# Moving the cluster similarities of the next head pair into the middle of each attention turn

## The chip, the cores and the metric

The kernel runs on one core of a Trainium2 chip. The metric is the device time of one execution in microseconds (us). A core has five engines that each work through their own instruction list in order and meet through semaphores: TensorE (PE in the profile, with its weight loads as PEld), VectorE (DVE), ScalarE (ACT), GpSimd (POOL) and SyncE (SP, which here only starts transfers). Three executions of the kernel before took 701.83, 703.33 and 704.82 us; the median is 703.33 us. The profiled execution spans 687.2 us on the core's own clock; the rest of a measured time lies outside that span.

## The reference

Two blocks in sequence. The attention block groups queries and keys by the nearest of 16 normalised centroids, and lets a query see only the keys of its own cluster. The second block sends every token to one of 8 experts.

```python
B, H, S, D = 4, 8, 768, 64            # 16 clusters
q_assign = argmax(einsum('bhsd,hcd->bhsc', q_n, c_n), -1)     # the clusters
k_assign = argmax(einsum('bhsd,hcd->bhsc', k_n, c_n), -1)
mask = q_assign[:, :, :, None] == k_assign[:, :, None, :]
scores = where(mask, q @ k.T / sqrt(D), -1e9)
attn = softmax(scores) ; x = (attn @ v) -> rows of (B*S, H*D) = (3072, 512)

logits = x @ w_gate                    # 8 experts, one per token
expert = argmax(logits) ; gate_w = softmax(logits)[expert]
y = gate_w * (relu(x @ w1[expert]) @ w2[expert])              # F = 1024
```

Everything is float32 at the inputs and the output.

## The kernel before

The attention works on 16 pairs of heads, called g = 0 to 15 (4 batches, 4 pairs each). One pair is one **turn** of the main loop. A turn has 12 units (2 halves of the queries, 6 blocks of keys). First come the 12 scores of the turn, then the point called `mid`, then the 12 products with V (`attend`), then the point called `end`. Other work is hung in at named places: `at(g, mid, f, ...)` means that `f` is written into the instruction lists at the middle of turn g; `at(g, 5, ...)` after score number 5; `at(g, UG + 5, ...)` after attend number 5 (UG is 12). Every engine runs its list in that order.

```python
def similar(g):                       # similarities of pair g to the 16 centroids
    ps = ps_o.tile(...) if g == 1 else wide()[:, 0, :]
    for t in range(4): nc.tensor.matmul(ps[32 rows of t, 0:384], lhsT=cblk[...], rhs=qk[g][...])
    sims[g] = ...; nc.vector.transpose(sims[g], ps[:, 0:HS])

def assign(g):                        # largest similarity, first of equals (1st part)
    nc.vector.tensor_reduce(mx, sim, op=max)
    nc.vector.tensor_tensor(sim, sim, mx, op=is_ge)
    (nc.gpsimd if g > 1 else nc.vector).tensor_tensor(sim, sim, first_c, op=mult)

def assign2(g):                       # 2nd part: a one-hot of the cluster
    nc.vector.tensor_reduce(top, rank, op=max)
    nc.vector.tensor_tensor(oh, rank, top, op=is_equal)
    nc.vector.transpose(sims[g], oh)

def put_by_scalar(g):                 # one-hots to the operand that masks the scores
    for half in range(2):
        for a in range(2):
            nc.scalar.copy(ohT[g][..., 0, cols], t[i])
            nc.scalar.activation(ohT[g][..., 1, cols], t[k], AF.Identity, scale=..., bias=...)

def score(u):                         # 12 per turn
    ps = ps_s.tile([P, 2, 512])       # pool of 3, also used by wide()
    2 matmuls (float32) of k and q  ; 2 matmuls (bf16) of ohT add the mask
    A[u] = ap.tile(...)               # pool of 12
    nc.scalar.activation(A[u], ps, AF.Exp, scale=D**-0.5)
    if g == NG - 2 and u % UG >= 3: later_sums.append((u, A[u]))   # turn 14 only
    else: add_up(u, A[u])             # T += A on VectorE; 10 instructions for 12 units

def attend(u):  2 matmuls (float32) O += v . A[u]
def finish(g, half):  nc.scalar.copy(XT[g][half], O)
def weigh(g):   # sums of weights (from T) and gate logits (from XT), 12 small matmuls, then VectorE and GpSimd
def keep(g, c0, c1):  nc.vector.transpose(xb, XT[g]); four stores of rows by GpSimd's queue
def turn_blocks(g):   two VectorE transposes of q and k
def choose(pool, part):  # 5 VectorE instructions: expert of every token
def count(part):         # 2 small matmuls of the result of choose, then a VectorE copy
def slots1 / one_hots1(i):   # places of the tokens, on VectorE (and GpSimd)
def tokens1 / spread1:   # small matmuls, then VectorE: the row numbers to gather
def turn_rows1(i):       # VectorE: divide and transpose the gathered rows (tile xu)
def first_half(0, ...):  # first expert matmuls, read xu; start after weigh(15)
...
at(-1, end, turn_blocks, 1)
for f in (similar, assign, assign2): at(0, 4, f, 1)
for g in range(NG):
    at(g, end, finish, g, 0) ; at(g, end, finish, g, 1)
    if g + 2 < NG:
        at(g, mid, turn_blocks, g + 2)
        at(g, end, similar, g + 2) ; at(g, end, assign, g + 2)
    if g < NG - 1:
        at(g, end, keep, g, 0, S) ; at(g + 1, mid, weigh, g)
        at(g, mid, put_by_scalar, g + 1)
    if g + 2 < NG: at(g, end, assign2, g + 2)
    if g % HP == HP - 1 and g < NG - 1:      # HP = 4: after each batch
        at(g + 1, mid, gate, g // HP) ; at(g + 1, end, gate2, g // HP) ; ...
at(12, end, choose, pl, front) ; at(13, mid, count, front)
at(13, end, slots1) ; at(13, end, one_hots1, 0) ; at(13, end, one_hots1, 1)
at(14, UG + 3, tokens1) ; at(14, UG + 3, sums_of_later, 2)
at(14, UG + 6, spread1) ; at(14, UG + 6, gather1, 0) ; at(14, UG + 6, sums_of_later, UG)
at(15, mid, gather1, 1) ; at(15, mid, turn_rows1, 0)
at(16, mid, weigh, 15) ; ... at(16, mid, first_half, 0, 0, FB // 4)
```

So before the change the similarities of pair g + 2 are made at the end of turn g, and their one-hots are put in place in the middle of turn g + 1: a whole turn lies between them and the scores that need them.

Of the kernel before, what the change touches and what calls it, by code (L numbers as in the profile page):

```python
# [8 lines left out]
F32 = mybir.dt.float32  # L9
# [3 lines left out]
AF = mybir.ActivationFunctionType  # L13
# [172 lines left out]
def kernel(  # L186
# [11 lines left out]
    nc = tc.nc  # L198
    B, H, S, D = q.shape
    C = centroids.shape[1]  # L200
    P = 128
# [4 lines left out]
    NG = B * HP  # L206
# [27 lines left out]
    def fetch1(e, i):  # L234
        w1 = wpool.tile([P, DB, F], F32, name=f"w1_{i % 2}")
        nc.sync.dma_start(out=w1, in_=moe_w1[bass.ds(e, 1)].rearrange("e (a p) f -> p (e a) f", p=P))
        return w1

    def fetch2(e, i):
        w2 = wpool.tile([P, FB, Dm], F32, name=f"w2_{i % 2}")  # L240
        nc.sync.dma_start(out=w2, in_=moe_w2[bass.ds(e, 1)].rearrange("e (a p) d -> p (e a) d", p=P))
        return w2
# [24 lines left out]
    ps_o = late.enter_context(tc.tile_pool(name="ps_o", bufs=2, space=PSUM))  # L267
# [9 lines left out]
    def wide():  # L277
        return pools["s"].tile([P, 2, 512], F32, name="sps")
# [4 lines left out]
    def bank():  # L283

        return wide()[:, 0, :] if "attention" in pools else ps_o.tile([P, 512], F32, name="O")
# [332 lines left out]
    for name, t0, n in (("f", 0, NF), ("b", NF, NQ)):  # L618
# [4 lines left out]
            keep=rte.tile([P, E, n], F32, name="keep_" + name),  # L623
# [112 lines left out]
    with ExitStack() as actx:  # L736
# [9 lines left out]
        pl = actx.enter_context(tc.tile_pool(name="places1", bufs=1))  # L746
# [54 lines left out]
        big = consts.tile([P, 2, 2], F32)  # L801
# [14 lines left out]
        ps = bank()  # L816
# [15 lines left out]
        for i in range(2):  # L832
            t = ohp.tile([P, 2, S], BF16, name=f"ohT{i}")
            nc.gpsimd.memset(t, 0.0)
            ohTs.append(t)
        for a in range(2):
            r = slice(a * D, (a + 1) * D)
# [31 lines left out]
        qk, sims, ohT = {}, {}, {}  # L869
# [37 lines left out]

        def similar(g):


            ps = ps_o.tile([P, 512], F32, name="O") if g == 1 else wide()[:, 0, :]
            for t in range(4):
                w, half = divmod(t, 2)
                nc.tensor.matmul(  # L914
                    ps[t * 2 * C : (t + 1) * 2 * C, 0:HS], lhsT=cblk[:, g % HP].rearrange("p a c -> p (a c)"),
                    rhs=qk[g][:, w, half * HS : (half + 1) * HS], start=True, stop=True,
                )


            sims[g] = asg.tile([P, HS], F32, name="sim")  # L920
            nc.vector.transpose(sims[g], ps[:, 0:HS])

        def groups_of(t):
            return t.rearrange("p (t c) -> p t c", c=C)

        def assign(g):

            sim = groups_of(sims[g])
            mx = asg.tile([P, G], F32, name="mx")
            nc.vector.tensor_reduce(mx, sim, axis=AX, op=ALU.max)  # L930
            nc.vector.tensor_tensor(sim, sim, mx.unsqueeze(2).to_broadcast([P, G, C]), op=ALU.is_ge)  # L931
            (nc.gpsimd if g > 1 else nc.vector).tensor_tensor(  # L932
                sim, sim, first_c[:, None, :].to_broadcast([P, G, C]), op=ALU.mult
            )

# [12 lines left out]
        def places(half, a):  # L948

            return slice(half * 32, half * 32 + 32), slice(a * D, a * D + 32), slice(half * HS, (half + 1) * HS)  # L950

        def put_by_scalar(g):

            t = sims.pop(g)
            ohT[g] = ohTs[g % 2]
            for half in range(2):
                for a in range(2):
                    i, r, cols = places(half, a)
                    k = slice(D + half * 32, D + half * 32 + 32)
                    nc.scalar.copy(ohT[g][r, 0, cols], t[i])  # L960
                    nc.scalar.activation(  # L961
                        ohT[g][r, 1, cols], t[k], AF.Identity, scale=big[k, a, 0:1], bias=big[k, a, 1:2]
                    )

        def put(g):

# [19 lines left out]
        A, T, O = {}, {}, {}  # L986
        XT = {}

        def where(u):
            g, r = divmod(u, 2 * NQ)  # L990
            return g, r // NQ, r % NQ

        def score(u):
            g, half, j = where(u)
            qs = slice(half * HS, (half + 1) * HS)
            ks = slice(j * P, (j + 1) * P)
            ps = ps_s.tile([P, 2, 512], F32, name="sps")
            for a in range(2):
                r = slice(a * D, (a + 1) * D)
                nc.tensor.matmul(ps[:, a, 0:HS], lhsT=qk[g][r, 1, ks], rhs=qk[g][r, 0, qs], start=True, stop=False)  # L1000
            for a in range(2):
                r = slice(a * D, (a + 1) * D)
                nc.tensor.matmul(ps[:, a, 0:HS], lhsT=ohT[g][r, 1, ks], rhs=ohT[g][r, 0, qs], start=False, stop=True)  # L1003
            A[u] = ap.tile([P, 2, HS], F32, name="A")
            nc.scalar.activation(A[u], ps[:, :, 0:HS], AF.Exp, scale=D**-0.5)  # L1005
            if g == NG - 2 and u % UG >= 3:
                later_sums.append((u, A[u]))
            else:
                add_up(u, A[u])
# [3 lines left out]
        def add_up(u, a_u):  # L1013
            g, half, j = where(u)
            if j == 0:
                last_a[0] = a_u
            elif j == 1:
                T[g, half] = tp_.tile([P, 2, HS], F32, name="T", bufs=4)
                nc.vector.scalar_tensor_tensor(
                    T[g, half], in0=last_a[0], scalar=1e-9 / P, in1=a_u, op0=ALU.add, op1=ALU.add  # L1020
                )
            else:
                nc.vector.tensor_tensor(T[g, half], T[g, half], a_u, op=ALU.add)  # L1023
# [110 lines left out]
        def at(n, part, f, *a):  # L1134
            jobs.setdefault((n, part), []).append((f, a))

        UG = 2 * NQ
# [3 lines left out]
        mid, end = "mid", "end"  # L1141
# [3 lines left out]
        at(-4, mid, load_next)  # L1145
        at(-4, end, turn, 0, 1)
        at(-3, mid, similar, 0)
        at(-3, mid, assign, 0)
        at(-3, mid, assign2, 0)
        at(-3, mid, put, 0)  # L1150
        at(0, 2, put_q, 0, 1)
        at(-2, end, idle_of, 20)
        at(-1, end, turn_blocks, 1)
        for f in (similar, assign, assign2):
            at(0, 4, f, 1)
        for g in range(NG):
            at(g, end, finish, g, 0)
            at(g, end, finish, g, 1)
            if g + 2 < NG:
                at(g, mid, turn_blocks, g + 2)  # L1160
                at(g, end, similar, g + 2)
                at(g, end, assign, g + 2)
            if g < NG - 1:
                at(g, end, keep, g, 0, S)
                at(g + 1, mid, weigh, g)
                at(g, mid, put_by_scalar, g + 1)
            if g + 2 < NG:
                at(g, end, assign2, g + 2)
            if g % HP == HP - 1 and g < NG - 1:
                at(g + 1, mid, gate, g // HP)  # L1170
                at(g + 1, end, gate2, g // HP)
                at(g + 1, end, keep_pads, g // HP)


        front = parts[0]
# [39 lines left out]
            layer1(g, (f0, f1))  # L1215

        n = NG - HP
        at(n, end, choose, pl, front)
        at(n + 1, mid, count, front)
        at(n + 1, end, slots1)  # L1220
        at(n + 1, end, one_hots1, 0)
        at(n + 1, end, one_hots1, 1)

        at(n + 2, UG + 3, tokens1)
        at(n + 2, UG + 3, sums_of_later, 2)
        at(n + 2, UG + 6, spread1)
        at(n + 2, UG + 6, gather1, 0)
        at(n + 2, UG + 6, sums_of_later, UG)
        at(n + 3, mid, gather1, 1)
        at(n + 3, mid, turn_rows1, 0)  # L1230

        n = NG
# [35 lines left out]
        for n in range(-4, NTURN + 2):  # L1268
            for i, x in enumerate(range(n * NB, (n + 1) * NB)):
                if 0 <= x < NU:  # L1270
                    score(x)
                run(n, i)
            run(n, mid)
            for i, x in enumerate(range(n * NB, (n + 1) * NB)):
                if 0 <= x < NU:
                    attend(x)
                run(n, NB + i)
            run(n, end)
# [8 lines left out]
    with tc.tile_pool(name="sm", bufs=1) as sm:  # L1287
        front, back = parts
# [19 lines left out]
        for part in parts:  # L1308
            n, over = part["n"], part["over"]
# [95 lines left out]
    g = groups[0]  # L1405
# [61 lines left out]
    with tc.If(more > 0):  # L1467
        nx = nc.values_load(xe[0:1, NX : NX + 1], min_val=0, max_val=NX)
        general = nc.values_load(xe[0:1, NX + 1 : NX + 2], min_val=0, max_val=1)
        with tc.If(nx > XU):  # L1470
            with ExitStack() as ectx:
# [3 lines left out]
                with tc.For_i(XU, nx, 1) as i:  # L1475
# [5 lines left out]
                    g = dict(  # L1481
                        n=[P], rows=N, w=(fetch1(ex, 0), fetch2(ex, 0)), gi=lambda j, i: gi[:, i : i + 1],
                        si=lambda j: gi[:, 4:5], apart=False,
                    )
# [37 lines left out]
```

## Time and profile before

| what | value |
|---|---|
| time, median of 3 | 703.33 us (701.83 to 704.82) |
| span of the profiled execution | 687.2 us |
| granted TensorE clock, mean | 0.995 |
| attention, turn 0 (first score to first score of turn 1) | 15.07 to 35.94 us |
| attention, one turn in the middle | 19.68 us |
| first expert matmul | 332.62 us |

The page of a profile gives, engine by engine, the share of the span in which it was busy; then a picture of the span in 40 slices; then the chain of waits that ended last; then the groups of instructions, each with its count, total, mean duration and what ended the idle time before it. The timeline gives instructions in order of their start, with the start first and the time taken second, both in us; equal neighbours are merged and `xN` says how many. A bracket at the end of a line gives idle time ahead of it and what ended it. PE records overlap (several small matmuls run side by side in parts of the array), so a row's pace is read from starts, not from durations.

### The profile page before, as it was taken

The numbers are of one execution on the slowest core, as the hardware profiler recorded it, in microseconds if no ns is written. First come the engines' busy times: TensorE is split into PE (matmuls) and PEld (weight loads), VectorE is DVE, ScalarE is ACT, GpSimd is POOL, SyncE is SP. The second block draws the span as 40 slices with busy tenths as digits, with TensorE's granted clock in tenths as the row PEclk, the third lists the DMA queues.
The fourth block names the chain that finished last, engine by engine and source line by source line (L and its number), as shares of the span: only waits on it lengthen the run. The fifth ranks groups of instructions, "written<-read, shape, count | busy, mean of one in ns | idle before, by whom it ended". The sixth has DMA issues, their size and how long they took to land.

```text
span 687.2 us, 11979 instructions
## 1 busy us (share of the span) xinstructions
PE 674.8 (98%) x4603; PEld 440.1 (64%) x4603; DVE 471.8 (69%) x740; ACT 310.6 (45%) x470; POOL 253.6 (37%) x327
## 2 busy tenths in 40 slices
PE   8999999999999999999999999999999999999994
PEld 7444444445454444555656789878788787888761
DVE  6887888779887778889666549576755767564300
ACT  3887777778877777785111031211113111131100
POOL 5022222122222221257816774547352563412101
PEclk9999999999999999999999999999999999999997
DMA  7566864997759643421435349586676866668440
GB/s 144 90 93 93 154 140 86 152 150 153 117 74 195 98 68 38 49 48 33 68 125 176 119 135 371 198 291 207 233 268 212 306 195 236 244 230 300 161 140 20
DMA packets 149540, 106.71 MB, mean 155 GB/s; under 512 B 115554, under 2 KB 119650, under 8 KB 149475
## 3 DMA queue, kind: packets, MB, share of 16 engines
q1 hardware_dynamic: 135266, 77.41, 42.9%
q0 software_dynamic: 8640, 19.63, 13.0%
q10 hardware_dynamic: 5568, 8.83, 4.3%
q8 instruction: 38, 0.62, 0.4%
q14 instruction: 28, 0.22, 0.1%
HBM read 93.06 MB, written 13.30 MB: 155 GB/s over the span
## 4 chain that ended last, share of the span: by engine, by line
PE 74%; issue 14%; POOL 6%; DVE 2%; DMA 1%; SPq 1%; POOLq 0%; ACTq 0%; ACT 0%; DVEq 0%
PE sps L1000 17%; PE O L1038 17%; PE sps L321 9%; PE sps L498 8%; PE sps L386 7%; PE sps L520 5%; PE sps L1003 4%; POOL xg L292 3%; PE sps L1060 3%; POOL out_dram L341 2%; PE sps L914 2%; DMA k_in<-in_k_dram 1%; PE sps L357 1%; DVE T L1023 1%; SPq L764 0%
## 5 line engine op out<-in xcount | busy, mean ns | idle before, releaser
L1005 ACT ACTIVATE A<-sps 128x768 f32<-128x768 f32 x192 | 153.7, 810 | 22.3 <-PE sps L1003 21.0
L292 POOL DMA_INDIRECT xg<-x_rows,g_idx x104 | 120.4, 1158 | 115.5 <-DVE xgT L308 81.1
L1000 PE MATMUL sps<-qk 64*128 64x384 f32 x768 | 157.0, 487 | 0.0
L1023 DVE TENSOR_TENSOR T<-T,A 128x768 f32<-128x768 f32 x128 | 122.6, 958 | 13.1
L1038 PE MATMUL O<-A,v_in 128*64 128x384 f32 x768 | 127.8, 488 | 0.0
L1000 PEld LDWEIGHTS sps<-qk 64*128 64x128 f32 x768 | 67.6, 187 | 48.7 <-issue 44.5
L1038 PEld LDWEIGHTS O<-A,v_in 128*64 128x64 f32 x768 | 53.6, 137 | 67.0 <-issue 65.0
L1003 PE MATMUL sps<-ohT 64*128 64x384 bf16 x384 | 63.6, 322 | 0.0
L386 PE MATMUL sps<-w,h_sb 128*128 128x512 f32 x144 | 63.1, 592 | 0.0
L341 POOL DMA_INDIRECT out_dram<-zo,s_idx x32 | 37.5, 1172 | 67.6 <-ACT zo L337 25.1
L321 PEld LDWEIGHTS sps<-xgT,w 128*128 128x128 f32 x448 | 51.0, 192 | 3.7 <-issue 3.7
L321 PE MATMUL sps<-xgT,w 128*128 128x128 f32 x448 | 51.3, 275 | 0.0
L1072 POOL COPY dens<-ls 128x12 f32<-128x12 f32 x16 | 3.6, 226 | 124.3 <-DVE ls L1068 124.3
L1091 POOL DMA_DIRECT2D x_rows<-xb x68 | 48.3, 718 | 2.1 <-issue 0.7
L932 POOL TENSOR_TENSOR sim<-sim,first_c 128x384 f32<-128x384 f32 x14 | 14.0, 1002 | 91.2 <-DVE sim L931 91.2
L386 PEld LDWEIGHTS sps<-w,h_sb 128*128 128x128 f32 x144 | 26.8, 190 | 30.6 <-issue 30.6
L961 ACT ACTIVATE ohT<-ohs,big 32x384 bf16<-32x384 bf16 x60 | 42.0, 700 | 0.8
L364 ACT COPY zc<-sps 32x512 f32<-32x512 f32 x24 | 13.9, 578 | 60.2 <-PE sps L357 60.0
L337 ACT COPY zo<-sps 128x512 f32<-128x512 f32 x12 | 7.0, 586 | 71.3 <-PE sps L386 65.5
L498 PEld LDWEIGHTS sps<-xs,w1s 128*128 128x128 f32 x288 | 36.0, 190 | 5.0 <-DVE xs L409 4.2
L498 PE MATMUL sps<-xs,w1s 128*128 128x144 f32 x288 | 37.9, 288 | 0.0
L331 ACT ACTIVATE h_sb<-sps 128x512 f32<-128x512 f32 (+1 forms) x18 | 9.6, 578 | 58.1 <-PE sps L321 58.1
(265 smaller groups left out, 953.3 us busy)
## 6 DMA issues: line engine op xcount, KB each, us to landing
w<-in_moe_w_dram SPq DMA_DIRECT2D x28, 2048.0 KB, 9.3
w<-in_moe_w_dram ACTq DMA_DIRECT2D x16, 512.0 KB, 4.5
v_in<-in_v_dram SPq DMA_DIRECT2D x16, 384.0 KB, 3.5
q_in<-in_q_dram SPq DMA_DIRECT2D x60, 96.0 KB, 4.0
k_in<-in_k_dram SPq DMA_DIRECT2D x60, 96.0 KB, 5.2
x_rows<-xb POOLq DMA_DIRECT2D x60, 96.0 KB, 5.3
xg<-x_rows,g_idx POOLq DMA_INDIRECT x104, 3.3
x_rows<-pad SPq DMA_DIRECT2D x64, 3.0 KB, 2.6
```

The source lines that it names most:

```text
L292: nc.gpsimd.indirect_dma_start(out=g["xg"][:, n, :], out_offset=None, in_=x_q[0 : 4 * g["rows"], :], in_offset=bass.IndirectOffsetOnAxis(a ...
L321: nc.tensor.matmul(o, lhsT=g["w"][0][:, c, fb * P : (fb + 1) * P], rhs=g["xT"][:, c, :cols], start=(c == 0), stop=(c == DB - 1),)
L341: ins = nc.gpsimd.indirect_dma_start(out=out[:, :], out_offset=bass.IndirectOffsetOnAxis(ap=g["si"](j)[0:m], axis=0), in_=zo[0:m], in_offs ...
L386: nc.tensor.matmul(zp, lhsT=g["h"][:, fb, j * P : (j + 1) * P], rhs=g["w"][1][:, fb, :], start=(fb == 0), stop=(fb == FB - 1),)
L498: nc.tensor.matmul(o, lhsT=a[:, c, f * P : (f + 1) * P], rhs=b[:, c, :], start=(c == 0), stop=(c == KH - 1),)
L961: nc.scalar.activation(ohT[g][r, 1, cols], t[k], AF.Identity, scale=big[k, a, 0:1], bias=big[k, a, 1:2])
L1000: nc.tensor.matmul(ps[:, a, 0:HS], lhsT=qk[g][r, 1, ks], rhs=qk[g][r, 0, qs], start=True, stop=False)
L1003: nc.tensor.matmul(ps[:, a, 0:HS], lhsT=ohT[g][r, 1, ks], rhs=ohT[g][r, 0, qs], start=False, stop=True)
L1005: nc.scalar.activation(A[u], ps[:, :, 0:HS], AF.Exp, scale=D**-0.5)
L1023: nc.vector.tensor_tensor(T[g, half], T[g, half], a_u, op=ALU.add)
L1038: nc.tensor.matmul(O[g, half][a * D : (a + 1) * D, 0:HS], lhsT=rows[g, "v"][:, a, j, :], rhs=a_[:, a, :], start=(j == 0), stop=(j == NQ - 1),)
L1091: nc.gpsimd.dma_start(out=x_d[b * S + c0 : b * S + c1, quad, hp * 32 : (hp + 1) * 32].rearrange("(n t) d -> t n d", t=32), in_=xb[quad * 3 ...
```

## The change

It makes the similarities of the next pair (g + 1) in the middle of turn g, directly ahead of the sums of weights (`weigh`), rather than those of pair g + 2 at its end. The clusters of pair g + 1 are then needed by the very next turn, so the chain to them is shortened: VectorE does all of it (the multiplication no longer goes to GpSimd), the last three additions of a turn wait until the chain is through, the copies on ScalarE are split in two halves, and the two result copies (`finish`) are moved, one between the halves, one behind the third score of the next turn. Some work of the later turns moves with it: `choose` from the end of turn 12 to attend 5 of turn 13, `count` from the middle to the end of turn 13, and `spread1`, the first gather and the sums that wait from attend 6 to attend 8 of turn 14.

```diff
 def similar(g):
-    ps = ps_o.tile([P, 512], F32, name="O") if g == 1 else wide()[:, 0, :]
+    ps = wide()[:, 0, :]
 def assign(g):
-    (nc.gpsimd if g > 1 else nc.vector).tensor_tensor(
+    nc.vector.tensor_tensor(
-def put_by_scalar(g):            # both halves at once
+def put_by_scalar(g, half):      # two copies and two activations
 # in score:
-            if g == NG - 2 and u % UG >= 3:
+            if g < NG - 1 and u % UG >= (3 if g == NG - 2 else UG - 3):
                 later_sums.append((u, A[u]))
 # the places:
-        for f in (similar, assign, assign2):
-            at(0, 4, f, 1)
         for g in range(NG):
-            at(g, end, finish, g, 0)
-            at(g, end, finish, g, 1)
+            if g == NG - 1:
+                at(g, end, finish, g, 0)
+                at(g, end, finish, g, 1)
+            else:
+                at(g + 1, 2, finish, g, 1)
+                at(g + 1, 2, keep, g, 0, S)
+                at(g, mid, similar, g + 1)
+                at(g, mid, assign, g + 1)
+                at(g, mid, assign2, g + 1)
+                at(g, mid, sums_of_later, 3 if g < NG - 2 else 0)
+                at(g, mid, put_by_scalar, g + 1, 0)
+                at(g, UG + 5, finish, g, 0)
+                at(g, UG + 5, put_by_scalar, g + 1, 1)
+            if g > 0:
+                at(g, mid, weigh, g - 1)
             if g + 2 < NG:
                 at(g, mid, turn_blocks, g + 2)
-                at(g, end, similar, g + 2)
-                at(g, end, assign, g + 2)
-            if g < NG - 1:
-                at(g, end, keep, g, 0, S)
-                at(g + 1, mid, weigh, g)
-                at(g, mid, put_by_scalar, g + 1)
-            if g + 2 < NG:
-                at(g, end, assign2, g + 2)
         ...
         n = NG - HP                                  # 12
-        at(n, end, choose, pl, front)
-        at(n + 1, mid, count, front)
+        at(n + 1, UG + 5, choose, pl, front)
+        at(n + 1, end, count, front)
         at(n + 1, end, slots1)
         ...
         at(n + 2, UG + 3, tokens1)
-        at(n + 2, UG + 3, sums_of_later, 2)
-        at(n + 2, UG + 6, spread1)
-        at(n + 2, UG + 6, gather1, 0)
-        at(n + 2, UG + 6, sums_of_later, UG)
+        at(n + 2, UG + 8, spread1)
+        at(n + 2, UG + 8, gather1, 0)
+        at(n + 2, UG + 8, sums_of_later, UG)
```

The computation is the same; no matmul is added or removed.

More of the change, by code (lines that the diff above doesn't have):

```diff
@@ L950, in places @@
             return slice(half * 32, half * 32 + 32), slice(a * D, a * D + 32), slice(half * HS, (half + 1) * HS)
-        def put_by_scalar(g):
-            t = sims.pop(g)
+        def put_by_scalar(g, half):
+            t = sims.pop(g) if half else sims[g]
             ohT[g] = ohTs[g % 2]
[L956 to L963, printed above, removed]
+            for a in range(2):
+                i, r, cols = places(half, a)
+                k = slice(D + half * 32, D + half * 32 + 32)
+                nc.scalar.copy(ohT[g][r, 0, cols], t[i])
+                nc.scalar.activation(
+                    ohT[g][r, 1, cols], t[k], AF.Identity, scale=big[k, a, 0:1], bias=big[k, a, 1:2]
+                )
         def put(g):
@@ L1153 @@
         at(-1, end, turn_blocks, 1)
-        for f in (similar, assign, assign2):
-            at(0, 4, f, 1)
         for g in range(NG):
-            at(g, end, finish, g, 0)
-            at(g, end, finish, g, 1)
+            if g == NG - 1:
[13 more added lines that the diff above has]
+                at(g, mid, weigh, g - 1)
             if g + 2 < NG:
                 at(g, mid, turn_blocks, g + 2)
-                at(g, end, similar, g + 2)
-                at(g, end, assign, g + 2)
-            if g < NG - 1:
-                at(g, end, keep, g, 0, S)
-                at(g + 1, mid, weigh, g)
-                at(g, mid, put_by_scalar, g + 1)
-            if g + 2 < NG:
-                at(g, end, assign2, g + 2)
+        for g in range(NG):
             if g % HP == HP - 1 and g < NG - 1:
```

## The prediction

> **What bounds the kernel now.** I read the busy shares first, then the waits of TensorE, then the timeline of one attention turn, then the timelines of VectorE and ScalarE where the change adds dependences. From the page, the engines' shares of the span:
>
> ```profile
> PE 674.8 (98%) x4603; PEld 440.1 (64%) x4603; DVE 471.8 (69%) x740; ACT 310.6 (45%) x470; POOL 253.6 (37%) x327
> ```
>
> PE is busy 98%; the waits of PE list four stalls, the longest 1.4 us, so almost none is left to take away. DVE's 69% is an average: over a middle turn (75.3 to 95.0) DVE is busy 17.4 of 19.7 us and ACT 15.4. These two have little room, and the change gives them deadlines. Now PE alone through one turn, from the timeline (start, time taken):
>
> ```profile
> 65.25 0.33 PE L1003 MATMUL sps<-ohT 64*128 64x384 bf16 x2
> 65.51 0.86 PE L1060 MATMUL sps<-T,one_row 128*32 128x192 f32 x16
> 66.18 0.51 PE L1060 MATMUL sps<-xT,wg 128*32 128x192 f32 x8
> 66.62 7.96 PE L1038 MATMUL O<-A,v_in 128*64 128x384 f32 x48
> 74.51 0.85 PE L914 MATMUL sps<-qk,cblk 128*32 128x384 f32 x8
> 75.29 0.92 PE L1000 MATMUL sps<-qk 64*128 64x384 f32 x4
> 76.04 0.33 PE L1003 MATMUL sps<-ohT 64*128 64x384 bf16 x2
> 76.20 0.81 PE L1000 MATMUL sps<-qk 64*128 64x384 f32 x4
> ```
>
> From starts: weigh takes 66.62 - 65.51 = 1.11, attend 7.89, similar 0.78; the next weigh starts at 85.18, so the scores take 9.89. Sum 19.67 us per turn, no hole. Each change of the array's tiling (64*128, 128*32, 128*64) leaves a small loss: mask to weigh 0.26 where mask to score is 0.16, so 0.10; weigh to attend 0.44 where eight such matmuls take 0.67/2, so 0.10. The first score after similar takes 0.75 to its mask, later ones 0.65.
>
> [...]
>
> **The change, part by part.**
>
> *1. One change of tiling less per turn.* Similar and weigh are both 128*32 and now adjacent. Before: attend to similar to score; after: attend to score. Eight similar matmuls at four side by side should take 0.645 (two score pairs at 0.3225 each); they take 0.78, so the change away costs about 0.13. Over turns 1 to 13: 13 x 0.13 = **-1.7 us**.
>
> *2. The start.* In turn 0 similar(1) sits between scores and similar(2) at the end waits for turn_blocks:
>
> ```profile
> 33.28 0.97 DVE L899 STREAM_TRANSPOSE qk<-q_in 128x768 f32<-128x768 f32 x1
> 34.18 0.94 DVE L899 STREAM_TRANSPOSE qk<-k_in 128x768 f32<-128x768 f32 x1
> ```
>
> PE's L914 there starts at 34.31 and lasts 1.70, not 0.85; turn 1 starts at 35.94. After: score 6 needs the buffer that exp 3 frees (ACT ends it at 20.65, then one exp each 0.80), so the scores end at about 25.6, similar ends at 26.35, attend takes 7.9, and turn 1 starts at 34.4: 1.55 gained. But DVE: blocks end at 19.24, the seven sums of units 1 to 8 end at 26.4, then the chain. In this trace the chain took 23.26 to 27.40 = 4.14 (seven instructions, all DVE for pair 1), so the one-hots are there at 30.65. ACT then needs 8 puts, which took 46.77 to 51.75 = 4.98, and one finish of 0.5: done at 36.1. The first exp wants to start 1.12 after the first score (75.29 to 76.41), at 35.5; it is 0.6 late, and the finish behind exp 2 leaves no slack for score 6. Net **-0.9 us**.
>
> *3. A turn in the middle: does the new chain fit?* Count from the first score, t = 0. Scores end and similar starts at 9.89; DVE can start 0.92 later (74.51 to 75.43), at 10.8. DVE's own load: exp 1 ends at 2.74; the sums of units 1 and 2, keep (0.9), the sums of 3, 4, 5, 7, 8 at 1.03 end at 10.8. Three sums wait, so DVE is just free. Chain 4.14: 15.0. Half of the puts 2.5: 17.5; finish 18.1 (attend 6 ended at about 15.6); second half 20.6. The next turn starts at 19.6 and its first exp wants ACT at 20.7. It fits by 0.1 to 0.2. In the next scores, finish behind exp 2 moves the end of exp 3 to 1.12 + 2.42 + 0.5 + 0.81 = 4.85 while score 6 wants its buffer at 4.94: just fits. DVE after the chain: three sums 3.1, weigh's transpose and reciprocal 0.6, turn_blocks 1.9, ending at 20.4, before it is wanted at 22.4. So PE still sets the pace; I allow **+0.5** over all turns for the margins. The multiplication (1.00 us on GpSimd, 0.56 on DVE) is in the 4.14.
>
> *4. Turns 4, 8 and 12* have the gate's small exp on ACT. Its input is now made behind turn_blocks, at 20.8, so ACT is free at 21.1 rather than 20.7: about 0.3 each, **+1.0 us**.
>
> *5. Turn 13: count waits.* Before, choose ran a turn early:
>
> ```profile
> 277.15 0.27 DVE L632 TENSOR_TENSOR sc<-lg,lmax 128x144 f32<-128x144 f32 x1
> ...
> 278.57 0.46 DVE L640 TENSOR_TENSOR_SCAN pr_f<-keep_f,sel_f 128x144 f32<-128x144 f32 x1
> ```
>
> and count ran unhindered at 283.48. Now choose is in DVE's list behind turn_blocks(15), free at 20.35; its five instructions took 277.15 to 279.03 = 1.9, so its result is there at 22.25. But count is the last PE work of turn 13, and PE reaches it at 19.6. TensorE stands still for **+2.65 us**; the two matmuls themselves (0.5) were there before.
>
> *6. Turns 14 to 16: DVE is late for the experts.* Before:
>
> ```profile
> 328.23 0.38 DVE L1068 STREAM_TRANSPOSE ls<-sps 128x192 f32<-128x192 f32 x1
> 328.63 0.23 DVE L1071 RECIPROCAL rd<-ls 128x12 f32<-128x12 f32 x1
> 329.00 1.51 DVE L305 TENSOR_TENSOR xg<-xg 128x1152 f32<-128x1152 f32 x1
> 330.55 1.38 DVE L308 STREAM_TRANSPOSE xu<-xg 128x1152 f32<-128x1152 f32 x1
> ```
>
> xu ends at 331.93 and PE's first expert matmul starts at 332.62: 0.7 us to spare. After, with t from turn 13's first score: count ends 22.95, cnt copied 23.15, slots1 and one_hots1 6.2 (297.39 to 303.59) to 29.35, two sums and keep to 32.3, wait for similar(15) to 33.8, chain to 37.9, weigh 0.6, indices 1.15 to 39.65, wait for spread1 at attend 8 to 41.6, its five instructions to 42.55, eight sums to 50.75, ten sums and keep of turn 15 to 61.9, then as above 3.86 to xu: 65.75. PE: turn 14 starts at 23.05, turn 15 at 43.65, weigh(15) at 62.6, so it wants xu at 63.7. **+2.05 us.** The gather (14.6 us of issue from 311.50, now from 42.6, so issued by 57.2) is in time.
>
> Behind that PE is again busy throughout and the shift passes on. Sum: -1.7 - 0.9 + 0.5 + 1.0 + 2.65 + 2.05 = **+3.6 us**; 703.3 + 3.6 = 706.9.
>
> **Rivals.** *(a) Only the gain shows.* If count and xu do not stall (DVE faster than I sum), -1.7 - 0.9 is left: 700.7. For it: someone moved choose, count and spread1 with care. Against: the order of DVE's list is fixed, and each duration is measured. *(b) The turn chain does not fit.* ACT's margin is 0.1 to 0.2 us. If semaphores or jitter add 0.3 per turn, ACT sets the pace, and 14 x 0.3 = 4.2 more gives 711. For it: margins of 0.1 in two places. Against: the waits I read already hold the semaphore times (27.40 to 27.49 from DVE to ACT). *(c) Taking GpSimd out of the chain and the interrupted scores help more than I think.* Against: both lay beside PE's work, GpSimd's wait was hidden by a whole turn.
>
> **Range and chances.** Gains sum to 2.6 and stalls to 6.2; either can be off by half. Rival (a) at one in seven puts the lower end at 701.5, rival (b) at one in seven the upper end at 711. The 2% limits are 689.3 and 717.4; no sum above reaches either. Faster by over 2%: 0.02; within 2%: 0.94; slower by over 2%: 0.04.
>
> **What would show each step right or wrong.** Step 1: turns of 19.5 to 19.6 us, weigh directly behind similar. Step 2: turn 1's first score near 34.4. Step 3: no repeated stall of PE on ACT (score 6) or on the mask's puts; if the turns are longer than 19.7, rival (b). Step 4: turns 5, 9 and 13 longer by 0.3. Step 5: PE idle ahead of L645 by 2 to 3 us, released by DVE. Step 6: PE idle ahead of the first expert matmul by about 2 us, released by DVE's xu. The prediction is wrong if 5 and 6 are absent, or if a stall recurs in every turn.

## The result, and the profile after

The changed kernel takes 710.40 us (median of 6) where the kernel before takes 702.97 us in the same comparison: a ratio of 1.0104, 95% interval 1.0081 to 1.0127. It is slower by about 1%, inside the range that was predicted, and for the reasons predicted in part.

Of the 16 us between the median of before, 703.33 us, and the span of its profile, 687.2 us, only some 1.8 lie outside the span: the profiled execution itself took 688.95 us, and the other executions of that comparison were some 14 us longer than it. So the span of the profile of after cannot be set beside that of before as it stands. Behind the first expert matmul the profile of after shows 370.1 us (710.1 - 339.97), that of before 354.6 us (687.2 - 332.62). Both kernels were profiled again later (runs e0 and e8 below): there each has 354.5 or 354.6 us behind that matmul, and the ratio is nearly the same, 1.0112 (1.0093 to 1.0130). So the expert part is the same in both, the 15 us come and go with the occasion, and all of the difference lies ahead of the first expert matmul, which moved from 332.62 to 339.97 us: **7.35 us**.

The page of after, the engines' busy time:

```profile
PE 681.6 (96%) x4603; PEld 444.8 (63%) x4603; DVE 478.4 (67%) x754; ACT 303.7 (43%) x470; POOL 239.8 (34%) x313
```

The busy time has hardly moved: GpSimd's 14 multiplications are gone from POOL and are found again on DVE (740 to 754 instructions). What is new stands in the waits of TensorE (us in total, times, longest):

```profile
PE sps L386 <- DVE h_sb L329: 3.8, 1, 3.8
PE sps L998 <- ACT A L1003: 3.6, 3, 1.8
PE sps L498 <- issue: 3.1, 6, 0.8
PE sps L645 <- DVE pr_f L640: 2.6, 1, 2.6
PE sps L321 <- DVE xu L308: 1.8, 1, 1.8
```

Before, none of these five was there. L386 and L498 lie in the expert part, among the 15 us, and are not in e8. L645 is the wait of count, L321 that of the first expert matmul for xu, both as predicted. L998, TensorE waiting for an exp of ScalarE to free a buffer, was not predicted at that size.

A middle turn from PE's timeline:

```profile
44.58 0.85 PE L913 MATMUL sps<-qk,cblk 128*32 128x384 f32 x8
45.25 0.83 PE L1058 MATMUL sps<-T,one_row 128*32 128x192 f32 x16
45.90 0.51 PE L1058 MATMUL sps<-xT,wg 128*32 128x192 f32 x8
46.34 7.96 PE L1036 MATMUL O<-A,v_in 128*64 128x384 f32 x48
54.23 0.92 PE L998 MATMUL sps<-qk 64*128 64x384 f32 x4
```

Similar takes 45.25 - 44.58 = 0.67, no longer 0.78, and the next similar starts at 64.12: the turn is 19.54 us long, where it was 19.68.

To see where the 7.35 us come from, take as the mark the start of weigh, the first L1060 (before) or L1058 (after) of each turn. At that mark both kernels have done the same matmuls. The last column is the same difference between the later profiles, e8 and e0.

| mark | before | after | after - before | what it adds | e8 - e0 |
|---|---|---|---|---|---|
| weigh of turn 1 | 45.83 | 45.25 | -0.58 | the start: -0.58 | +0.28 |
| weigh of turn 13 | 282.37 | 283.67 | +1.30 | turns 1 to 12: +1.88 | +1.28 |
| weigh of turn 14 | 302.59 | 308.09 | +5.50 | count: +4.20 | +5.47 |
| weigh of turn 16 | 331.51 | 336.99 | +5.48 | nothing | +5.44 |
| first expert matmul | 332.62 | 339.97 | +7.35 | xu: +1.87 | +7.30 |

The terms of count (+4.19) and of xu (+1.86) come back in the second pair. The start does not: its sign changes, so it is no more than the scatter between two executions. The turns 1 to 12 add +1.00 there, because ScalarE's loss in turns 5 and 9 varies; that the two totals agree within 0.05 us is partly chance.

The +1.88 of turns 1 to 12 is two things. Ten of those twelve turns are 19.54 us long. The other two, turns 5 and 9, are 21.72 and 21.31 us: 3.95 us lost in two places, against some 2.1 us gained in all twelve. In e8 these two turns take 21.30 and 20.83 us, a loss of 3.05, and the gain of the twelve is again 2.1.

Turn 5, from ScalarE's timeline (ACTq is its queue of transfers):

```profile
129.61 0.70 ACT L959 ACTIVATE ohT<-ohs,big 32x384 bf16<-32x384 bf16 x1
131.65 1.34 ACTq L1257 DMA_DIRECT2D w<-in_moe_w_dram  x2
133.09 0.48 ACT L1044 COPY xT<-O 128x384 f32<-128x384 f32 x1 [2.78 <-DMA q_in<-in_q_dram]
133.58 0.51 ACT L958 COPY ohT<-ohs 32x384 bf16<-32x384 bf16 x1
```

The first half of the cluster copies ends at 130.31. Then ScalarE stands for 2.78 us until its two transfers of early expert weights are issued; only then come finish and the second half, which ends at 136.04. The first exp wanted to start about 1.1 us after the first score at 132.39, and TensorE waits 1.84 us for the buffers. In turn 4 the same two issues start at 108.31, with the first copy, and take 0.82 us beside the copies.

### The profile page after: what moved, and what is told of

It reads as the page before. It is cut to its first block, busy times and chain, and to the rows that moved or that the text cites. A ratio compares the mean times of both kernels' runs of the same rounds, so it can differ in the third digit from the quotient of the medians.

```text
span 710.1 us, 11931 instructions
## 1 busy us (share of the span) xinstructions
PE 681.6 (96%) x4603; PEld 444.8 (63%) x4603; DVE 478.4 (67%) x754; ACT 303.7 (43%) x470; POOL 239.8 (34%) x313
## 4 chain that ended last, share of the span: by engine, by line
PE 54%; issue 15%; POOL 7%; DVE 7%; DMA 6%; SPq 3%; another core or an unknown queue 3%; ACT 3%; ACTq 0%; POOLq 0%; DVEq 0%
PE sps L998 12%; PE O L1036 9%; PE sps L498 8%; PE sps L321 6%; PE sps L386 5%; PE sps L520 5%; POOL xg L292 4%; SPq L1124 3%; PE sps L1001 3%; POOL out_dram L341 2%; PE sps L913 2%; DMA q_in<-in_q_dram 1%; PE sps L357 1%; DMA x_rows<-pad 1%
## 5 line engine op out<-in xcount | busy, mean ns | idle before, releaser
L998 PE MATMUL sps<-qk 64*128 64x384 f32 x768 | 159.1, 492 | 3.8 <-ACT A L1003 3.6
L1003 ACT ACTIVATE A<-sps 128x768 f32<-128x768 f32 x192 | 149.7, 817 | 8.2 <-PE sps L1001 8.1
L998 PEld LDWEIGHTS sps<-qk 64*128 64x128 f32 x768 | 67.9, 188 | 53.3 <-issue 31.7
L386 PE MATMUL sps<-w,h_sb 128*128 128x512 f32 x144 | 63.4, 593 | 3.8 <-DVE h_sb L329 3.8
L958 ACT COPY ohT<-ohs 32x384 bf16<-32x384 bf16 x60 | 30.6, 510 | 63.3 <-DVE ohs L945 62.6
L321 PEld LDWEIGHTS sps<-xgT,w 128*128 128x128 f32 x448 | 51.0, 192 | 3.7 <-issue 3.7
L321 PE MATMUL sps<-xgT,w 128*128 128x128 f32 x448 | 51.3, 275 | 0.0
L386 PEld LDWEIGHTS sps<-w,h_sb 128*128 128x128 f32 x144 | 26.7, 190 | 34.8 <-issue 30.1
L1017 DVE SCALAR_TENSOR_TENSOR T<-A 128x768 f32<-128x768 f32 x32 | 30.6, 955 | 24.7 <-ACT A L1003 24.7
L498 PEld LDWEIGHTS sps<-xs,w1s 128*128 128x128 f32 x288 | 36.2, 190 | 5.5 <-DVE xs L409 4.2
L498 PE MATMUL sps<-xs,w1s 128*128 128x144 f32 x288 | 38.5, 289 | 0.0
```

The lines of the kernel that those rows point to most:

```text
L321: nc.tensor.matmul(o, lhsT=g["w"][0][:, c, fb * P : (fb + 1) * P], rhs=g["xT"][:, c, :cols], start=(c == 0), stop=(c == DB - 1),)
L386: nc.tensor.matmul(zp, lhsT=g["h"][:, fb, j * P : (j + 1) * P], rhs=g["w"][1][:, fb, :], start=(fb == 0), stop=(fb == FB - 1),)
L498: nc.tensor.matmul(o, lhsT=a[:, c, f * P : (f + 1) * P], rhs=b[:, c, :], start=(c == 0), stop=(c == KH - 1),)
```

## The experiments

### Both kernels once more

e0 is the kernel before, e8 the kernel after, neither edited.

> The kernel before, unchanged, profiled once more. The profiled execution of before on record took 689 us, while its timed ones took 701 to 705. Theory A: the 14 us between them lie in the expert part, behind the first expert matmul, and the kernel after has them too (its profile has 370 us there, the one of before 355); then this profile has its first expert matmul near 332.6 us, and usually some 370 us behind it, and the true difference between the kernels is the 7.35 us by which the first expert matmul moved (332.62 to 339.97). Theory B: the change itself made the expert part slower by 15 us; then this profile again shows some 355 us behind the first expert matmul.

> The kernel after, unchanged, on the chip of the next three. In run e0 the kernel before took 687.5 us and had 354.6 us behind the first expert matmul, so the 15 us that the profile of after had more there went with the chip or the hour. Theory A: after again has 354.6 us behind its first expert matmul near 339.7 us, so the two kernels differ only in the attention part, by 7 to 7.5 us (ratio 1.010). Theory B: the change does something to the expert part that shows on some chips; then this profile has more than 360 us there.

e0 took 687.5 us. Its first expert matmul is at 331.18 and 354.6 us lie behind it: theory A of e0, that a slow expert part is the usual one, is wrong. In this and all later comparisons, on three chips, the kernel before took 687.5 to 689.0 us. e8 took 696.33 us beside 688.18, ratio 1.0112 (1.0093 to 1.0130), with its first expert matmul at 338.48 and 354.5 us behind it. Theory A of e8 holds: the kernels differ in the attention part alone, here by 338.48 - 331.18 = 7.30 us. The waits are those of after again: 2.7 us on exps, 2.60 on count, 1.8 on xu. Why the first comparison was 14 to 15 us slower for both is left open; it does not touch the ratio. All ratios below are against the kernel before in their own comparison, and are to be read beside 1.0112 and 1.0104. Each profile is one execution.

### Who issues the early weights (e1), and when the small stores go (e9)

```diff
 # e1, in early(e, i): 16 transfers in turns 2 to 9
-                nc.scalar.dma_start(
+                nc.sync.dma_start(
 # e9, alone: the row stores of batches 0 and 1 behind turns 10 and 11, not 4 and 8
-                at(g + 1, end, keep_pads, g // HP)
+                at({0: 10, 1: 11}.get(g // HP, g + 1), end, keep_pads, g // HP)
```

> The kernel after, with the 16 early weight transfers issued from SyncE and not from ScalarE; nothing else changed. Theory A (issue from ScalarE): in turns 5 and 9 ScalarE's queue is held up by these two issues, which now stand between the halves of the cluster copies, so finish and the second half start some 2.5 us late and TensorE waits for the first exps (1.84 and 1.43 us). Then the turns 4 to 5 and 8 to 9 shrink from 21.7 and 21.3 us to 19.54, together 3.9 us, and the time falls from 710.4 to about 706.5. Theory B (the gate's work on VectorE and ScalarE at the end of turns 4 and 8, step 4 of the prediction, is what delays ScalarE): both turns stay above 21 us and the time stays at 710.

> The kernel after, with the 16 small row stores of the first two batches (SyncE, 3 KB each, 9.9 to 10.3 us of issue) put at the end of turns 10 and 11 rather than 4 and 8. ScalarE still issues the early weights between its halves. Theory A: ScalarE's issue is held up only where SyncE, behind those stores, issues its loads late and so at the same time as ScalarE; then turns 5 and 9 are 19.54 us, as with the issue moved to SyncE (ratio near 1.006). Theory B: something else in turns 5 and 9 holds ScalarE (for instance the state after the gate); then both stay above 20.5 us and the ratio stays at 1.011.

e1: ratio 1.0063 (1.0050 to 1.0077), and all middle turns are 19.54 us, 5 and 9 too (similar of turns 4, 5 at 102.56, 122.09; of 9, 10 at 200.25, 219.79). Theory A holds; the ratios give 2.8 to 3.4 us less for the 3.9 expected, near the 3.05 us that e8 loses in these turns. e9: ratio 1.0055 (1.0038 to 1.0072), again every middle turn 19.54 us. In e9 ScalarE still issues between its halves, in the same place of its list; turn 5 there:

```profile
128.06 0.51 ACT L958 COPY ohT<-ohs 32x384 bf16<-32x384 bf16 x1 [4.12 <-DVE ohs L945]
128.07 0.82 ACTq L1257 DMA_DIRECT2D w<-in_moe_w_dram  x2
128.59 0.70 ACT L959 ACTIVATE ohT<-ohs,big 32x384 bf16<-32x384 bf16 x1
```

The issue starts with the first copy and takes 0.82 us, so nothing waits. Together the two runs show the cause: the 16 small stores occupy SyncE's queue for some 10 us (in after from 115.12 to 125.39), its loads of q and k follow late and bunched (128.98 to 137.96, behind the middle of turn 5 at 122.74; in e9 from 113.67 to 120.14, ahead of it at 122.96), and an issue of ScalarE that falls into that bunch starts late and goes slowly (in after 1.34 us behind the last copy in turn 5 and 0.67 in turn 9, taking 1.34 and 1.60 us). Either taking ScalarE out of it or moving SyncE's stores, and with them the bunch, away restores the turn. Theory B (the gate) is out: e9 leaves the gate where it was. What exactly slows the issue stays open. e9 moves the stores and the bunch together, and being issued at the same moment is not all of it: in turn 6 of after, ScalarE's issue took 1.42 us though SyncE's last load had been issued 1.7 us before (149.57 and 147.85).

### Choose and count where they were (e2)

```diff
-        at(n + 1, UG + 5, choose, pl, front)
-        at(n + 1, end, count, front)
+        at(n, end, choose, pl, front)
+        at(n + 1, mid, count, front)
```

> The kernel after, with choose at the end of turn 12 and count in the middle of turn 13, where they were before the change. Theory A: the stall of 2.60 us ahead of count goes, and with it the 3.4 us at half the granted TensorE clock that follow (1.7 us lost), so 4.3 us less; choose then stands ahead of the sums of turn 13 on VectorE and costs 0.5 to 1 us there. Time about 706.5 to 707. Theory B (the slow scores behind count have another cause, such as the work of slots1 on VectorE): only 2.6 us less, and the slow scores with a clock of 0.5 remain at the start of turn 14. In both, the wait for xu (1.80 us) stays within 0.5 us of what it was, because VectorE and TensorE both move forward.

Ratio 1.0049 (1.0035 to 1.0063), so 3.8 to 4.3 us less than after: theory A. The wait on L645 is gone, and from the weigh of turn 10 to that of turn 14 it is 78.70 us (224.56 to 303.26) where after takes 83.03 (225.06 to 308.09): four turns of 19.54 and count's own 0.54. The expected loss of 0.5 to 1 us by choose at the end of turn 12 did not come: it would lie in that stretch, and nothing is left over there. VectorE starts the chain of turn 13 at 284.42, 1.9 us after similar began instead of 0.9, and TensorE shows no wait for it. The wait for xu stays at 1.8 us, as both theories had it.

### TensorE kept busy in front of count (e5)

```diff
+        at(n + 1, end, idle_of, 10)
         at(n + 1, end, count, front)
```

> The kernel after, with 10 idle matmuls (some 2.4 us, their result unused) between the last attend of turn 13 and count. The wait for choose stays, but TensorE is busy in it. Theory A: the slow scores at the start of turn 14 (1.5 us a score, granted clock 0.50 to 0.55) come from the 2.60 us in which TensorE stood still; then the clock stays at 1.00 there, the scores take 0.81 us each from the second on, and turn 13 to turn 14 shortens from 24.42 us to about 22.7. Theory B: they come from work that starts at the same time (slots1 on VectorE, the transfers): the clock is again near 0.5 for some 3 us.

In after, TensorE stands for 2.60 us ahead of count, and the scores behind it are slow:

```profile
295.32 0.36 PE L645 MATMUL sps<-pr_f,lt_strict 128*128 128x8 f32 x2 [2.60 <-DVE pr_f L640]
...
296.75 1.39 PE L998 MATMUL sps<-qk 64*128 64x384 f32 x4
298.24 1.50 PE L998 MATMUL sps<-qk 64*128 64x384 f32 x4
299.84 1.03 PE L998 MATMUL sps<-qk 64*128 64x384 f32 x4
300.86 0.81 PE L998 MATMUL sps<-qk 64*128 64x384 f32 x4
```

The windows of after give the granted clock of these stretches (the third number from the end, after the busy times of PE, PEld, DVE, ACT and POOL):

```profile
295.30:296.70 1.40, 1.38 (x10) 1.03 (x12) 0.69 (x3) 0.00 (x0) 0.00 (x0) 1.00 0.09 31
296.70:298.20 1.50, 1.50 (x10) 0.73 (x8) 1.40 (x5) 0.81 (x1) 0.00 (x0) 0.55 0.00 0
298.20:299.80 1.60, 1.60 (x8) 0.83 (x8) 1.43 (x8) 0.81 (x1) 0.34 (x1) 0.50 0.00 0
```

With the idle matmuls (e5):

```profile
295.51 2.50 PE L811 MATMUL sps<-ident 128*128 128x128 f32 x20
298.19 0.36 PE L645 MATMUL sps<-pr_f,lt_strict 128*128 128x8 f32 x2 [0.18 <-DVE pr_f L640]
...
299.61 0.81 PE L998 MATMUL sps<-qk 64*128 64x384 f32 x4
300.42 0.81 PE L998 MATMUL sps<-qk 64*128 64x384 f32 x4
```

Count starts just as long after the last attend, but the scores take 0.81 from the second on, the clock is 1.00 in all windows from 293 to 306, and from similar of turn 13 to similar of turn 14 it is 22.73 us where after has 24.42. In this execution that is what theory A said: no standstill, no slow scores, 1.7 us less.

By itself it proves less than it seems. In e9, count waits as in after, nothing fills the wait, and the scores are fast all the same:

```profile
291.60 0.36 PE L645 MATMUL sps<-pr_f,lt_strict 128*128 128x8 f32 x2 [2.61 <-DVE pr_f L640]
...
292.11 0.92 PE L998 MATMUL sps<-qk 64*128 64x384 f32 x4
293.02 0.81 PE L998 MATMUL sps<-qk 64*128 64x384 f32 x4
```

The five scores behind these two take 0.81 us too (up to 297.87), and from similar to similar it is 22.73 us, just as in e5. e7 has 2.75 us of standstill at this place, and the scores behind it take 0.92 and then 0.81 us; both ran on the same chip, on which e7 does have slow stretches in other turns (below). So seven profiles have the standstill, and in five of them there is a further loss behind it. In after and e8 the clock is at 0.50 there. From the weigh of turn 10 to that of turn 14 it is 83.03 us in after, e8 and e1, 83.02 in e3 and 85.34 in e6, but 81.35 in e9; of the three of the changed kernel that lack the standstill, e5 takes 81.34 us with its idle matmuls, e2 78.70 and e4 78.71. The measured time of e2 says the same for most executions: taking the standstill away gained 3.8 to 4.3 us, more than its own 2.60. The standstill is what the loss of 1.7 us goes with, but it does not always bring it, and what decides is open.

The execution of e5 as a whole was no faster, 697.44 us (one run), because turn 9 cost more in this execution than in others: TensorE waits 2.77 us for an exp (to 218.09), the clock is 0.59 from 218 to 222, and the turn takes 24.27 us.

### Sums in VectorE's idle stretches (e3)

```diff
-            if g < NG - 1 and u % UG >= (3 if g == NG - 2 else UG - 3):
+            if g < NG - 1 and u % UG >= (4 if g == NG - 2 else UG - 3):
         at(n + 2, UG + 3, tokens1)
+        at(n + 2, UG + 3, sums_of_later, 2)
```

> The kernel after, with one sum more made at once in turn 14 and two of the waiting sums put behind tokens1, so that VectorE sums where it now waits for similar(15) (about 1.4 us) and for spread1 (about 1.9 us). No work is added or removed. Theory A (step 6: VectorE's list is what makes xu late, and its two idle stretches in turn 14 are part of it): xu is ready some 2.5 to 3 us earlier and the wait of 1.80 us ahead of the first expert matmul goes; time about 708.6. Theory B (the wait is for the gathered rows, a transfer, not for VectorE's work): the wait stays, and the multiplication of the gathered rows shows idle time ahead of it; time 710.4.

The wait of the first expert matmul is gone. VectorE of e3:

```profile
332.18 1.54 DVE L305 TENSOR_TENSOR xg<-xg 128x1152 f32<-128x1152 f32 x1
333.75 1.38 DVE L308 STREAM_TRANSPOSE xu<-xg 128x1152 f32<-128x1152 f32 x1
```

xu is ready at 335.13 and TensorE starts on it at 336.37, straight behind weigh at 335.93. So VectorE's list, with its two idle stretches, made xu late, not the gathered rows. In the measured time this one edge is hard to see: ratio 1.0099 (1.0083 to 1.0115). The wait of 1.8 us is 0.26% of the time; in the ratios 0.05 to 0.13 of a point appears, and the intervals of e3 and of after overlap. The profile shows the wait gone, the timing alone would not.

### The multiplication on GpSimd again (e6), and no sums waiting (e7)

```diff
 # e6
-            nc.vector.tensor_tensor(
+            (nc.gpsimd if g > 1 else nc.vector).tensor_tensor(
                 sim, sim, first_c ...
 # e7, alone
-            if g < NG - 1 and u % UG >= (3 if g == NG - 2 else UG - 3):
+            if g == NG - 2 and u % UG >= 3:
-                at(g, mid, sums_of_later, 3 if g < NG - 2 else 0)
```

> The kernel after, with the multiplication of assign on GpSimd again, as before the change. The chain to the clusters is longer by 0.49 us (1.68 us rather than 1.19 from is_ge to the second reduction). Theory A (step 3: the chain fits by 0.1 to 0.2 us): ScalarE is late for the first exp of every turn by about 0.3 us and TensorE waits at the fourth or seventh score, 0.1 to 0.3 us in each of 13 turns, 1.5 to 3.5 us in all; middle turns of 19.65 to 19.85 us. Theory B (the chain has slack): middle turns stay at 19.54 us and the time stays that of after.

> The kernel after without the three waiting sums: in turns 0 to 13 every sum is made in its place, ahead of the chain to the clusters; turn 14 as it was. The chain starts 3.1 us later (3 x 1.03). Theory A: the first exps of the next turn come 2.5 to 2.9 us late, and TensorE stands 1.8 to 2.6 us in every turn 1 to 14[...]: 28 to 50 us more than after, middle turns of 21.5 to 23 us. Theory B (run e6 showed that a chain 0.49 us longer costs a middle turn nothing; the chain may have more slack than that): under 10 us more.

e6: ratio 1.0150 (1.0132 to 1.0167), some 2.6 us slower than after in e8's comparison. That is the amount of theory A, but not by its path. Ordinary middle turns stay at 19.54 us, although the chain is 0.49 us longer: that much is absorbed. The loss comes in turns 4, 8 and 12 (19.75 us each, where the gate's exp of 0.24 us stands ahead of the first exp on ScalarE) and at count: the wait there grows from 2.60 to 3.08 us, and similar to similar from 24.42 to 26.52 us, because the matmuls behind it are slow for longer: from count at 294.70 (0.57 us for 0.36) and the first score at 295.62 (1.65 us) until 301.86, where in after it is from 296.75 to 300.86. So VectorE alone is worth having in the places with other work, and nothing in a plain turn.

e7: 728.01 us (one run) against 696.33 for after: 31.7 us more, in the range of theory A (what that range holds above 14 waits of 2.6 us was an estimate). Turns 1 to 8 alternate, about 23.7 and 21.0 us; turns 9 to 12 take 22.1 to 22.2. From its timeline, a turn of the first kind:

```profile
61.69 0.92 PE L998 MATMUL sps<-qk 64*128 64x384 f32 x4 [1.85 <-ACT A L1003]
...
63.80 1.50 PE L998 MATMUL sps<-qk 64*128 64x384 f32 x4
```

TensorE stands 1.85 us for the exp and then runs scores at 1.50 us, with a granted clock of 0.58 between 62.6 and 66.7. In the turn that follows it stands 1.07 us and the clock stays at 1.00. In turns 9 to 12 it stands 1.85 to 1.99 us each time, and the scores behind take 0.92 and then 0.81 to 0.88 us. Without the three waiting sums the one-turn chain makes TensorE stand in every turn; the chain's slack in a plain turn lies between 0.49 us and 3.1 us.

### All three losses taken away (e4)

The edits of e1, e2 and e3 together.

> The kernel after with the three edits together: early weights issued from SyncE, choose and count where they were before, two sums and one in the idle stretches of VectorE in turn 14. If the three losses are the whole of it and independent: 7.35 less 3.95 (turns 5 and 9), 4.2 (count and the clock) and 1.8 (xu) leaves -2.6 us against before, ratio 0.996; every middle turn 19.54 us, no wait of TensorE over 0.5 us between the first score and the first expert matmul. If the losses hide one another (a stall taken away gives back a later one), the ratio stays at or above 1.000.

685.99 us against 688.18: ratio 0.9969 (0.9957 to 0.9981), 2.2 us faster than the kernel before. The sum gave 2.6, of which 0.58 was the start that the second pair did not show. The waits of TensorE that are left (e4):

```profile
PE sps L811 <- POOL ident masks.py:199: 1.4, 1, 1.4
PE sps L386 <- ACT hs L331: 0.6, 1, 0.6
PE sps L913 <- DVE qk L886: 0.6, 1, 0.6
PE sps L998 <- ACT A L1003: 0.4, 1, 0.4
PE sps L1001 <- ACT ohT L979: 0.2, 1, 0.2
```

L811 and L913 come before the first score, L386 in the expert part. All turns from 2 to 12 are 19.54 us, and the first expert matmul is at 329.68, where e0 has 331.18; from the weigh of turn 1 on, e4 takes 2.21 us less than e0. The losses were independent as far as these numbers tell: none gave its time back elsewhere.

## Why the prediction was right or wrong

The sum was +3.6 us and came out at +7.35 in the profile and +7.4 in the time. Direction and class were right, and so were the two stalls; about half of the loss was missing. That 710.4 us still lies inside the range is luck: the upper end of 711 was set for rival (b), which did not occur.

**Step 1 (one change of tiling less).** Right: 19.68 to 19.54, so 0.14 a turn where 0.13 was predicted. Before, three turns of the gate were 0.13 longer still, and that went too: some -2.1 us over turns 1 to 12.

**Step 2 (the start).** The times were right, the sum was not. Turn 1 starts at 34.23 (predicted 34.4) and ScalarE ends its copies late, at 36.16 (36.1). But turn starts are not the same mark in the two kernels: before, turn 0 held two similars, after, it holds one, and the other turns up in turn 14. At the weigh of turn 1 the gain is 0.58 us, of which 0.30 was there at the first score already (15.07 to 14.77). From the first score on it is 0.28, and in the second pair (e0, e8) a loss of 0.11: no gain outside the scatter where -0.9 was predicted.

**Step 3 (the chain fits).** Right in the result: no stall in a plain turn. Its sums rest on the profile of before: in the turn from 75 to 95 us VectorE and ScalarE follow the order of the code, and VectorE's ten sums start 1.02 us apart (79.99 to 90.19) where the step takes 1.03. The allowance of +0.5 was not needed. The margin of 0.1 to 0.2 us for the first exp was read well (ScalarE has 0.22 us to spare ahead of it in e9), but TensorE does not need that exp at once: in e6 it starts 1.42 us after the first score (73.04 to 74.46) rather than 1.12, and TensorE does not wait in a plain turn. Rival (b) is refuted.

**Step 4 (turns with the gate).** Wrong. I gave +1.0 us to the gate's exp; turns 4, 8 and 12 are 19.54 us, a loss of nothing. In turn 4 of after the gate's exp makes the first exp start 1.24 us after the first score (112.85 to 114.09) rather than 1.12, and TensorE does not wait. The sign that I had named for this step, turns 5 and 9 longer, did appear, but by another cause. The loss is one turn later, 3.95 us, in ScalarE's issue of the early weights (3.05 us in e8), which the step does not name at all. The profile of before had shown it, in turn 5:

```profile
130.04 1.72 ACTq L1255 DMA_DIRECT2D w<-in_moe_w_dram  x2
131.85 0.48 ACT L1046 COPY xT<-O 128x384 f32<-128x384 f32 x1 [1.36 <-DMA q_in<-in_q_dram]
```

There the wait of 1.36 us stood behind all eight copies, in front of a finish with time to spare. The change put four copies and finish behind it, with a deadline. I read ScalarE's list in turns 1 and 3 and took them for all.

**Step 5 (count).** The stall was right, 2.60 us for 2.65. What failed is the size of the term: a standing TensorE was taken to lose its own time only. In after it lost 1.7 us more by the clock (24.42 us from similar to similar, 22.73 in e5 and e9); four of the other six profiles with this standstill have such a loss too, and e2, e4 and e5, without the standstill, show none. The granted clock behind the standstill was 0.50 to 0.55 in after, but in e9 one of 2.61 us was followed by scores of 0.81; what decides it is not shown.

**Step 6 (xu).** Right: 1.80 us for 2.05, by the mechanism named, as e3 shows. It let turn 14 start 23.05 us after turn 13, where it started after 22.73; both lists begin there, so little follows from it.

**Rival (a)**, only the gain shows, was refuted by the two stalls; e4 shows what it would have been worth, 0.3%. Rival (c), that the start and the shorter chain help more than thought, shows nowhere: a chain longer by 0.49 us costs a plain turn nothing (e6). Put together for the first pair: -0.6 + (-2.1 + 3.95) + 4.2 + 1.87 = +7.3.

## What to carry to other kernels

When work moves into a shorter deadline, read every instance of the list it moves into, not one typical turn: transfers issued from an engine that also computes are part of its list, and a wait that cost nothing behind the work (1.36 us in turn 5 of before) made that turn 2.18 us longer in front of it (2.78 us in after). Where a matmul depends on another engine's list, add up that list to the matmul's place; if TensorE would stand still there, do not count the standstill alone: 2.60 us of it went with 4.2 us lost in after and e8, while 2.61 us in e9 were followed by no slow scores. Move the work to where nothing waits (e2), or keep TensorE busy (e5). And compare two schedules at a mark where both have done the same work, and in more than one pair of profiles.

## What the runs showed of the hardware that was not expected

- A standstill of TensorE of 2.60 us was followed by about 3 us at a granted clock of 0.50 to 0.55 (scores of 1.50 us for 0.81) in after and likewise in e8 (0.50 to 0.54), and e1 and e3 lose as much time there (83.03 and 83.02 us for the four turns, 83.03 in after); one of 3.08 us in e6 was followed by matmuls that are slow for some 7 us (294.70 to 301.86). Behind one of 2.61 us in e9 and one of 2.75 us in e7 the scores take 0.92 and then 0.81 us. In e7 alone, of nine standstills of 1.85 to 1.99 us four were followed by scores of 1.50 us (at a clock of 0.58 behind the one at 61.69) and five were not (0.88 at most behind the first score). In these runs the length alone does not decide it.
- Issues of transfers from ScalarE can be slow. Two weight issues take 0.82 us in a quiet turn; in turns 5 and 9, amid SyncE's loads, they take 1.34 and 1.60 us in after, and they start up to 1.3 us after the last copy ahead of them. ScalarE's computing instructions behind them in the list wait for that, 2.78 us in turn 5. The reverse is not shown: in e1 four loads of q took SyncE 6.35 us (from 124.75) with no issue of ScalarE beside them, where they took 2.65 in e9.
- Both kernels took 14 to 15 us more in the first comparison than in all later ones. In the profile of after they lie between 395 and 435 us, in the expert part, where TensorE is busy 1.21 of 5 us in one stretch (400 to 405) and the clock falls to 0.50 in another (425 to 430). The cause is open.
